# Key decay terms of an attention kernel: from tiles spread over the partitions to one more matmul per score tile

## The chip, the cores and the metric

The kernel runs on one core of a Trainium2 chip. The metric is the device time of one execution in microseconds; the times given are medians of several runs, and the profile is of one further execution.

## What is computed

Three layers follow each other: causal attention with a decay (4 batches, 8 heads, 576 positions, head width 64), a mixture of 8 experts with one expert per token (2304 tokens), and a feed-forward layer. Only the attention is touched by the change:

```python
scores = scale * np.matmul(q, k.transpose(0, 1, 3, 2))
log_f = np.log(np.clip(f, 0.0001, 1.0))
cum = np.cumsum(log_f, axis=-1)
decay = cum[:, :, :, None] - cum[:, :, None, :]
scores = np.where(causal, -1000000000.0, scores + decay)
scores = scores - np.max(scores, axis=-1, keepdims=True)
attn = np.exp(scores)
attn = attn / (np.sum(attn, axis=-1, keepdims=True) + 1e-09)
return np.matmul(attn, v).astype(np.float32)
```

The query's own term, `cum[:, :, :, None]`, is the same for a whole row and falls out of the softmax. What remains is a row over the keys, `-cum`, that is added to every row of a head's scores.

## The kernel before

**Units.** The heads are taken in 16 pairs (`gp`, four per batch), and each pair in six units (`SUB`, line 541): units 0 and 1 are the fourth row block of each head (128 queries by 512 keys), units 2 and 3 the third and the first block of one head (384 and 128 keys), unit 4 the second blocks of both heads (256 each), unit 5 the last 64 queries of both heads, stacked on the partitions, by 512 and 64 keys. 96 units run through a software pipeline (line 1322). Its step n issues `scores(n+2)`, `parts_hi` and `parts_lo` of n-1, `maxima(n+2)`, `values(n-3)`, `exps(n+1)` and `turn(n)`, and after them what the table `side` holds for the step: loads, splits, transposes and stores at steps that the numbers of `PRM` set by hand. Every engine's order, that of the DMA queue of SP too, is the order of these calls, and each engine works in order.

**Scores.** `scores` (line 552, TensorE) puts a unit's tile into one PSUM buffer `s`: for every piece of keys one matmul with the high half (`wcc`, line 566) and one with halves swapped (`yw`, line 567), then `identb` times `maskb` for the causal mask on the diagonal block (line 568). Queries and keys come in half a batch at a time (`hb`, eight of them, four heads each): `prep_load`, `prep` (split into two float16 parts), `prep_turn` (DMA transposes, line 313, into `wcc`) and `prep_swap` (line 353: two DMAs that write `yw`, the keys with the 64-row halves exchanged).

**Decay.** At the start `cum_log` and `cum_sums` (lines 424 to 440) compute -8 times the running sum for the 32 heads as a 32x576 float32 tile, and `cum_store` writes it to `cumd` in HBM. `cb_spread(gp)` (line 388) then reads it back for each pair, spread over partitions: `cb` holds both heads' first 512 values on all 128 partitions, `c4` one head's 576 on the lower and the other's on the upper 64. It is issued eight steps before the pair begins (line 921), 48 DMAs in all.

**Reductions.** `maxima` (line 599, VectorE) adds the spread tile to the scores, scales by -1/8, writes the float32 tile `e` and takes the row minimum into `nm` (line 608; lines 614 and 618 for unit 5). `exps` (ScalarE, line 631) makes `t`, `turn` transposes it on TensorE into `pt` (line 643), `parts_hi` (ScalarE) and `parts_lo` (VectorE, line 659) split that into `p`, and `values` (lines 694 and 708) multiplies with V. `normal` and `rows` (lines 720 and 736) make the finished rows `nat`, which `rows_store` writes to `xs` (line 769); there are two buffers of `nat`.

**Others in the same steps.** The routing of a batch (line 783 on, with scatters of 4-byte indices into `ids`), loads and splits of one expert's weights, and three early slots of 128 tokens of that expert (`xgt`, `hs`, `ht`) run between the units. Behind step 98 come the other expert slots and the feed-forward layer, which need the transfers of weights and are not touched.

Of the kernel before, what the change touches and what calls it, by code (L numbers as in the profile page):

```python
# [92 lines left out]
def kernel(  # L93
# [22 lines left out]
    P = 128  # L116
# [26 lines left out]
    cumd = dram.tile([B * H, S], F32, name="cumd")  # L143
# [5 lines left out]
    mask4 = const.tile([P, 64], BF16, name="mask4")  # L149
    ones16 = const.tile([P, P], F16, name="ones16")  # L150
# [237 lines left out]
    def cb_spread(gp):  # L388

        cb = cbp.tile([P, 2, 512], F32, tag="cb", name="cb")  # L390
        nc.sync.dma_start(out=cb, in_=cumd[2 * gp:2 * gp + 2, 0:512].partition_broadcast(P))

        c4 = cbp.tile([P, S], F32, tag="cb4", name="cb4")
        for a in range(2):
            nc.sync.dma_start(out=c4[64 * a:64 * a + 64, :], in_=cumd[2 * gp + a, :].partition_broadcast(64))
        cbs[gp] = (cb, c4)

    def identities():
        make_identity(nc, identf)
        nc.gpsimd.memset(maskb, 0.0)  # L400
        mh = maskb.rearrange("p (a c) -> p a c", a=2)
        nc.gpsimd.affine_select(
            out=mh, in_=mh, pattern=[[-1, 2], [-2, 64]], base=0, channel_multiplier=1,
            compare_op=ALU.is_ge, fill=-8.0e9,
        )
        nc.gpsimd.memset(mask4, 0.0)
        nc.gpsimd.affine_select(
            out=mask4, in_=mask4, pattern=[[-1, 64]], base=0, channel_multiplier=1,
            compare_op=ALU.is_ge, fill=-8.0e9,
        )  # L410
# [20 lines left out]
    def cum_sums():  # L431
# [8 lines left out]
        cum["cs"] = cs  # L440

    def cum_store():
        nc.sync.dma_start(out=cumd, in_=cum["cs"])
# [108 lines left out]
    def scores(u):  # L552
# [3 lines left out]
        h0 = 2 * (pr % 2)  # L556
        if SUB[x] is not None:
            ps = ps_s.tile([P, 512], F32, tag="s", name="s")
            for a, i, c0 in SUB[x]:
                w = i * P + P  # L560
                h = h0 + a
                lhs = t[:, i, 0, h, :]
                for (k0, kw, r0), (_, _, r1) in zip(keys(t[:, :, 1, h], i), keys(yt[:, :, h], i)):
                    last = k0 + kw == w
                    o = ps[:, c0 + k0:c0 + k0 + kw]
                    nc.tensor.matmul(o, lhsT=lhs, rhs=r0, start=True, stop=False)  # L566
                    nc.tensor.matmul(o, lhsT=lhs, rhs=r1, start=False, stop=not last)  # L567
                nc.tensor.matmul(ps[:, c0 + w - P:c0 + w], lhsT=identb, rhs=maskb, start=False, stop=True)  # L568
            U[u] = [ps]
        else:  # L570
            pb = ps_s.tile([P, 64], F32, tag="s", name="sb")
            pa = ps_s.tile([P, 512], F32, tag="s", name="sa")
            lhs = [t[:, 4, 0, h0 + a, 0:64] for a in range(2)]
            for r in range(2):
                for a in range(2):
                    h = h0 + a
                    rhs = t[:, 4, 1, h, 0:64] if r == 0 else yt[:, 4, h, 0:64]
                    nc.tensor.matmul(pb[64 * a:64 * a + 64, :], lhsT=lhs[a], rhs=rhs, start=(r == 0), stop=False)
# [4 lines left out]
            for z in range(2):  # L583
                for r in range(2):
                    for a in range(2):
                        k0, kw, rhs = keys(t[:, :, 1, h0 + a] if r == 0 else yt[:, :, h0 + a], 3)[z]
                        nc.tensor.matmul(
                            pa[64 * a:64 * a + 64, k0:k0 + kw], lhsT=lhs[a], rhs=rhs, start=(r == 0), stop=(r == 1)
# [10 lines left out]
    def maxima(u):  # L599
        gp, x = divmod(u, NU)  # L600
        cb, c4 = cbs[gp]
        e = ep.tile([P, S], F32, tag="e", name="e")
        nm = nmp.tile([P, 2], F32, tag="nm", name="nm")
        if SUB[x] is not None:
            ps, = U[u]
            for y, (a, i, c0) in enumerate(SUB[x]):
                w = i * P + P
                nc.vector.tensor_tensor_reduce(  # L608
                    out=e[:, c0:c0 + w], in0=ps[:, c0:c0 + w], in1=cb[:, a, 0:w], scale=-1.0 / 8.0, scalar=3.0e38,
                    op0=ALU.add, op1=ALU.min, accum_out=nm[:, y:y + 1],  # L610
                )
        else:
            pa, pb = U[u]
            nc.vector.tensor_tensor_reduce(  # L614
                out=e[:, 512:S], in0=pb, in1=c4[:, 512:S], scale=-1.0 / 8.0, scalar=3.0e38,
                op0=ALU.add, op1=ALU.min, accum_out=nm[:, 1:2],
            )
            nc.vector.tensor_tensor_reduce(
                out=e[:, 0:512], in0=pa, in1=c4[:, 0:512], scale=-1.0 / 8.0, scalar=nm[:, 1:2],
                op0=ALU.add, op1=ALU.min, accum_out=nm[:, 0:1],  # L620
# [297 lines left out]
    for gp in range(B * NPAIR):  # L918
        o = PRM["gp" + str(gp)]
        if gp > 0:  # L920
            at(6 * gp - 8, cb_spread, gp)
# [379 lines left out]
    cb_spread(0)  # L1301
# [443 lines left out]
```

## Time and profile before

| what | value |
|---|---|
| median of 3 runs | 973.28 us (970.16 to 973.96) |
| profiled execution | 972.13 us, its span 970.4 us |
| TensorE busy | 799.5 us (82%), 5373 matmuls |
| VectorE busy | 513.6 us (53%) |
| ScalarE busy | 346.9 us (36%) |
| GpSimd busy | 339.4 us (35%) |
| mean granted TensorE clock | 0.92 |
| DMA traffic | 116.12 MB in 233,424 packets |

The busy times are sums over the whole span; a matmul's time runs from its start to its modelled end, so matmuls that follow closely overlap. A DMA share is the mean busy share of the 16 DMA engines; it exceeds 1 where an engine has several packets in flight. A wait is the idle time of an engine just before an instruction, put down to what ended it. In the views TensorE is PE (its weight loads PEld), VectorE DVE, ScalarE ACT, GpSimd POOL, and SPq the sequencer of SyncE, which issues most DMAs.

### The profile page before, as it was taken

Reading aid. Unit: us, or ns where it says so; the run is one execution under the profiler, and the core shown is the slowest. Engines: PE = TensorE matmul, PEld = TensorE weight load, DVE = VectorE, ACT = ScalarE, POOL = GpSimd, SP = SyncE. Lnnn points to the kernel's source line nnn. Section 1 sums busy time; section 2 is a strip of 40 time slices with the busy share of each in tenths; the row PEclk is TensorE's granted clock in tenths of the full one; section 3 lists DMA queues with packets and bytes.
Section 4 is the critical chain, followed back from the end, with each engine's and each line's share of the span. In section 5 each row is a group of like instructions: output and inputs, shape, how many; then the busy total and the mean of one; then the engine's idle time right before and its main releaser. Section 6 shows DMA issues by size and latency. Waiting matters only on the chain. (4 is left out here: it accounts for less than half of the span.)

```text
span 970.4 us, 15407 instructions
## 1 busy us (share of the span) xinstructions
PE 799.5 (82%) x5373; PEld 445.4 (46%) x5373; DVE 513.6 (53%) x1231; ACT 346.9 (36%) x670; POOL 339.4 (35%) x383
## 2 busy tenths in 40 slices
PE   4676663665788878497998889999999999999995
PEld 3565552553556543143443337444444444444442
DVE  5776573764765644558899578935005304501500
ACT  4676453643655442344545333312102101201200
POOL 3333252234232442454555434534114303411410
PEclk9887796779879989799999899999999999999998
DMA  9999999999999279799998936202000200000000
GB/s 186 194 179 195 186 149 161 211 195 162 170 179 142 39 134 163 150 267 204 238 242 217 228 84 163 60 22 44 12 33 1 43 33 12 1 23 22 1 22 22
DMA packets 233424, 116.12 MB, mean 120 GB/s; under 512 B 193587, under 2 KB 214592, under 8 KB 233346
## 3 DMA queue, kind: packets, MB, share of 16 engines
q1 hardware_dynamic: 227810, 100.25, 58.2%
q0 software_dynamic: 5536, 14.86, 5.0%
q8 instruction: 45, 0.74, 0.3%
q14 instruction: 33, 0.27, 0.1%
HBM read 62.05 MB, written 15.56 MB: 80 GB/s over the span
## 5 line engine op out<-in xcount | busy, mean ns | idle before, releaser
L1647 PE MATMUL a<-x,wi 128*128 128x512 f16 x768 | 167.4, 380 | 0.0
L1652 DVE TENSOR_SCALAR t<-a,al 128x512 f32<-128x512 f32 (+1 forms) x80 | 55.7, 696 | 205.2 <-PE a L1647 204.4
L1647 PEld LDWEIGHTS <-wi 128*128 128x128 f16 x960 | 94.5, 99 | 98.6 <-issue 6.0
L1669 PEld LDWEIGHTS <-g 128*128 128x128 f16 x864 | 84.5, 98 | 104.1 <-issue 2.4
L1210 PE MATMUL y<-wcc,ht 128*128 (+1 forms) x456 | 110.3, 398 | 20.0 <-DMA ht<-hs 19.1
L1175 PE MATMUL h<-wcc,xgt 128*128 (+1 forms) x456 | 109.4, 396 | 20.2 <-POOL wcc L1377 14.5
L1660 POOL TENSOR_TENSOR g<-t,g 128x512 f16<-128x512 f32 (+1 forms) x80 | 85.6, 1072 | 113.8 <-ACT g L1659 110.9
L643 PE MATMUL pt<-identf,t 128*128 128x128 f32 x384 | 72.2, 318 | 61.3 <-ACT t L631 37.5
L1669 PE MATMUL o<-wo,g 128*128 128x512 f16 x540 | 119.5, 379 | 0.0
L1659 ACT ACTIVATE g<-t 128x512 f16<-128x512 f32 (+1 forms) x80 | 46.8, 586 | 154.7 <-DVE t L1655 150.0
L659 DVE SCALAR_TENSOR_TENSOR p<-pt,p 128x512 f16<-128x512 f32 x96 | 65.5, 683 | 43.9 <-ACT p L652 42.7
L631 ACT ACTIVATE t<-e,nm 128x512 f32<-128x512 f32 (+2 forms) x144 | 81.2, 601 | 15.7 <-DVE nm L608 8.9
L1210 PEld LDWEIGHTS <-ht 128*128 128x128 f16 x480 | 48.2, 101 | 83.4 <-DMA ht<-hs 26.1
L1175 PEld LDWEIGHTS <-xgt 128*128 128x128 f16 x480 | 47.9, 101 | 79.2 <-issue 22.0
L643 PEld LDWEIGHTS pt<-identf,t 128*128 128x128 f32 x384 | 47.4, 160 | 66.8 <-ACT t L631 55.1
L1669 PE MATMUL o<-wob,g 128*128 128x512 f16 x324 | 73.2, 379 | 1.8 <-POOL wob L1455 1.6
L1676 POOL DMA_INDIRECT out_dram<-ob,tka x18 | 17.6, 977 | 153.5 <-ACT ob L1674 153.5
L608 DVE CUSTOM_DVE_ANT_0 e<-s,cb 128x512 f32<-128x512 f32 (+3 forms) x128 | 58.2, 481 | 22.0 <-PE s L568 18.6
L567 PE MATMUL s<-yw,wcc 128*128 128x256 f16 (+1 forms) x192 | 50.7, 293 | 22.5 <-DMA yw<-wcc 22.5
L1674 ACT ACTIVATE ob<-o 128x512 f32<-128x512 f32 x18 | 10.8, 598 | 160.9 <-PE o L1669 160.9
L652 ACT ACTIVATE p<-pt 128x512 f16<-128x512 f32 x96 | 56.3, 587 | 7.3 <-PE pt L643 3.1
L566 PE MATMUL s<-wcc 128*128 128x256 f16 (+1 forms) x192 | 52.4, 292 | 6.1 <-DVE nm L614 2.5
(305 smaller groups left out, 1136.6 us busy)
## 6 DMA issues: line engine op xcount, KB each, us to landing
cb<-cumd SPq DMA_DIRECT2D x16, 512.0 KB
raw<-in_moe_w_in_dram SPq DMA_DIRECT2D x16, 512.0 KB
raw<-in_moe_w_out_dram SPq DMA_DIRECT2D x16, 512.0 KB
cb<-cumd SPq DMA_DIRECT2D x32, 144.0 KB
yw<-wcc SPq DMA_DIRECT2D x14, 320.0 KB
kn<-in_k_dram SPq DMA_DIRECT2D x16, 256.0 KB
qn<-in_q_dram SPq DMA_DIRECT2D x32, 128.0 KB
vn<-in_v_dram SPq DMA_DIRECT2D x16, 256.0 KB
```

What stands on the lines that cost most here:

```text
L566: nc.tensor.matmul(o, lhsT=lhs, rhs=r0, start=True, stop=False)
L608: nc.vector.tensor_tensor_reduce(out=e[:, c0:c0 + w], in0=ps[:, c0:c0 + w], in1=cb[:, a, 0:w], scale=-1.0 / 8.0, scalar=3.0e38, op0=ALU.ad ...
L631: nc.scalar.activation(out=natural(t[:, c0:c0 + w]), in_=halves(e[:, c0:c0 + w]), func=AF.Exp, scale=-1.0, bias=nm[:, y:y + 1])
L643: nc.tensor.transpose(pt[:, c * P:(c + 1) * P], e[:, c * P:(c + 1) * P], identf)
L652: nc.scalar.activation(out=p[:, 0, 0:512], in_=U[u][0], func=AF.Copy, scale=SP)
L659: nc.vector.scalar_tensor_tensor(out=p[:, 1, 0:512], in0=U[u][0], scalar=SP, in1=p[:, 0, 0:512], op0=ALU.mult, op1=ALU.subtract)
L1175: nc.tensor.matmul(hps, lhsT=xgt[:, kk, l, :], rhs=m1(m, kk, cs_), start=(kk == 0 and y == 0), stop=(kk == KD - 1 and y == 2),)
L1210: nc.tensor.matmul(yps, lhsT=ht[:, kk // (KF // 2), l, kk % (KF // 2), :], rhs=m2(m, kk), start=(kk == 0 and y == 0), stop=(kk == KF - 1 a ...
L1647: nc.tensor.matmul(hps[:, 0:n], lhsT=wi[:, mm, kk, m * P:(m + 1) * P], rhs=x2[:, l, kk, 0:n], start=(kk == 0 and y == 0), stop=(kk == KD - ...
L1652: nc.vector.tensor_scalar(out=t[:, 0:n], in0=hps[:, 0:n], scalar1=0.0, scalar2=al[:, m:m + 1], op0=ALU.min, op1=ALU.mult)
L1660: nc.gpsimd.tensor_tensor(out=g[:, 1, 0:n], in0=t[:, 0:n], in1=g[:, 0, 0:n], op=ALU.subtract)
L1669: nc.tensor.matmul(ops, lhsT=g[:, l, t * P:(t + 1) * P], rhs=wo[m // (KH - LATE)][:, mm, m % (KH - LATE), :], start=(m == 0 and y == 0), s ...
```

## The change

The decay row is no longer added by VectorE from a spread tile. `cum_sums` splits it into three bfloat16 parts (`c3`: cast, subtract, cast, subtract, cast), `cumd` holds these, and `cb_load(hb)` brings 3 rows of four heads (3x4x576 bfloat16) for half a batch at once, at step `6 * gp - 12` for even `gp`. In `scores` a matmul with `one3` (3x128 ones) as weights and the three parts as moving operand opens every tile's accumulation, over the whole width. The reductions become `tensor_scalar` instructions with the scores as their only tensor.

```diff
--- before.py
+++ after.py
@@ -140,13 +140,14 @@
     ys = dram.tile([N, YW], F16, name="ys")
     G0 = 256
     ids = dram.tile([(E * ROWS + 1) * P, 1], I32, name="ids")
-    cumd = dram.tile([B * H, S], F32, name="cumd")
+    cumd = dram.tile([B * H, 3, S], BF16, name="cumd")
 
     identf = const.tile([P, P], F32, name="identf")
     identb = const.tile([P, P], BF16, name="identb")
     identh = const.tile([P, P], F16, name="identh")
     maskb = const.tile([P, P], BF16, name="maskb")
     mask4 = const.tile([P, 64], BF16, name="mask4")
+    one3 = const.tile([3, P], BF16, name="one3")
     ones16 = const.tile([P, P], F16, name="ones16")
     before16 = const.tile([P, P], F16, name="before16")
     ef = const.tile([P, E], F32, name="ef")
@@ -385,15 +386,11 @@
 
     cbs = {}
 
-    def cb_spread(gp):
-
-        cb = cbp.tile([P, 2, 512], F32, tag="cb", name="cb")
-        nc.sync.dma_start(out=cb, in_=cumd[2 * gp:2 * gp + 2, 0:512].partition_broadcast(P))
-
-        c4 = cbp.tile([P, S], F32, tag="cb4", name="cb4")
-        for a in range(2):
-            nc.sync.dma_start(out=c4[64 * a:64 * a + 64, :], in_=cumd[2 * gp + a, :].partition_broadcast(64))
-        cbs[gp] = (cb, c4)
+    def cb_load(hb):
+
+        cb = cbp.tile([3, 4, S], BF16, tag="cb", name="cb")
+        nc.sync.dma_start(out=cb, in_=cumd[4 * hb:4 * hb + 4].rearrange("h r s -> r h s"))
+        cbs[hb] = cb
 
     def identities():
         make_identity(nc, identf)
@@ -403,6 +400,7 @@
             out=mh, in_=mh, pattern=[[-1, 2], [-2, 64]], base=0, channel_multiplier=1,
             compare_op=ALU.is_ge, fill=-8.0e9,
         )
+        nc.gpsimd.memset(one3, 1.0)
         nc.gpsimd.memset(mask4, 0.0)
         nc.gpsimd.affine_select(
             out=mask4, in_=mask4, pattern=[[-1, 64]], base=0, channel_multiplier=1,
@@ -437,10 +435,16 @@
             out=halves(cs[:, 0:512]), in0=natural(cu[:, 0:512]), scalar1=-8.0, scalar2=None, op0=ALU.mult
         )
         nc.vector.tensor_scalar(out=cs[:, 512:S], in0=cu[:, 512:S], scalar1=-8.0, scalar2=None, op0=ALU.mult)
-        cum["cs"] = cs
+
+        c3 = ep.tile([BH, 3, S], BF16, tag="c3", name="c3", bufs=1)
+        for r in range(3):
+            nc.vector.tensor_copy(c3[:, r], cs)
+            if r < 2:
+                nc.vector.tensor_tensor(out=cs, in0=cs, in1=c3[:, r], op=ALU.subtract)
+        cum["c3"] = c3
 
     def cum_store():
-        nc.sync.dma_start(out=cumd, in_=cum["cs"])
+        nc.sync.dma_start(out=cumd, in_=cum["c3"])
 
     sets = {}
 
@@ -554,28 +558,37 @@
         b, pr = divmod(gp, NPAIR)
         t, yt = xy[2 * b + pr // 2], yw[2 * b + pr // 2]
         h0 = 2 * (pr % 2)
+        cb = cbs[2 * b + pr // 2]
         if SUB[x] is not None:
             ps = ps_s.tile([P, 512], F32, tag="s", name="s")
             for a, i, c0 in SUB[x]:
                 w = i * P + P
                 h = h0 + a
                 lhs = t[:, i, 0, h, :]
+                nc.tensor.matmul(ps[:, c0:c0 + w], lhsT=one3, rhs=cb[:, h, 0:w], start=True, stop=False)
                 for (k0, kw, r0), (_, _, r1) in zip(keys(t[:, :, 1, h], i), keys(yt[:, :, h], i)):
-                    last = k0 + kw == w
                     o = ps[:, c0 + k0:c0 + k0 + kw]
-                    nc.tensor.matmul(o, lhsT=lhs, rhs=r0, start=True, stop=False)
-                    nc.tensor.matmul(o, lhsT=lhs, rhs=r1, start=False, stop=not last)
+                    nc.tensor.matmul(o, lhsT=lhs, rhs=r0, start=False, stop=False)
+                    nc.tensor.matmul(o, lhsT=lhs, rhs=r1, start=False, stop=False)
                 nc.tensor.matmul(ps[:, c0 + w - P:c0 + w], lhsT=identb, rhs=maskb, start=False, stop=True)
             U[u] = [ps]
         else:
             pb = ps_s.tile([P, 64], F32, tag="s", name="sb")
             pa = ps_s.tile([P, 512], F32, tag="s", name="sa")
             lhs = [t[:, 4, 0, h0 + a, 0:64] for a in range(2)]
+            for a in range(2):
+                c = cb[:, h0 + a]
+                nc.tensor.matmul(
+                    pb[64 * a:64 * a + 64, :], lhsT=one3[:, 0:64], rhs=c[:, 512:S], start=True, stop=False
+                )
+                nc.tensor.matmul(
+                    pa[64 * a:64 * a + 64, :], lhsT=one3[:, 0:64], rhs=c[:, 0:512], start=True, stop=False
+                )
             for r in range(2):
                 for a in range(2):
                     h = h0 + a
                     rhs = t[:, 4, 1, h, 0:64] if r == 0 else yt[:, 4, h, 0:64]
-                    nc.tensor.matmul(pb[64 * a:64 * a + 64, :], lhsT=lhs[a], rhs=rhs, start=(r == 0), stop=False)
+                    nc.tensor.matmul(pb[64 * a:64 * a + 64, :], lhsT=lhs[a], rhs=rhs, start=False, stop=False)
             for a in range(2):
                 nc.tensor.matmul(
                     pb[64 * a:64 * a + 64, :], lhsT=identb[:, 0:64], rhs=mask4, start=False, stop=True
@@ -585,7 +598,7 @@
                     for a in range(2):
                         k0, kw, rhs = keys(t[:, :, 1, h0 + a] if r == 0 else yt[:, :, h0 + a], 3)[z]
                         nc.tensor.matmul(
-                            pa[64 * a:64 * a + 64, k0:k0 + kw], lhsT=lhs[a], rhs=rhs, start=(r == 0), stop=(r == 1)
+                            pa[64 * a:64 * a + 64, k0:k0 + kw], lhsT=lhs[a], rhs=rhs, start=False, stop=(z == 1 and r == 1)
                         )
             U[u] = [pa, pb]
 
@@ -598,26 +611,25 @@
 
     def maxima(u):
         gp, x = divmod(u, NU)
-        cb, c4 = cbs[gp]
         e = ep.tile([P, S], F32, tag="e", name="e")
         nm = nmp.tile([P, 2], F32, tag="nm", name="nm")
         if SUB[x] is not None:
             ps, = U[u]
             for y, (a, i, c0) in enumerate(SUB[x]):
                 w = i * P + P
-                nc.vector.tensor_tensor_reduce(
-                    out=e[:, c0:c0 + w], in0=ps[:, c0:c0 + w], in1=cb[:, a, 0:w], scale=-1.0 / 8.0, scalar=3.0e38,
-                    op0=ALU.add, op1=ALU.min, accum_out=nm[:, y:y + 1],
+                nc.vector.tensor_scalar(
+                    out=e[:, c0:c0 + w], in0=ps[:, c0:c0 + w], scalar1=-1.0 / 8.0, scalar2=3.0e38,
+                    op0=ALU.mult, op1=ALU.min, accum_out=nm[:, y:y + 1],
                 )
         else:
             pa, pb = U[u]
-            nc.vector.tensor_tensor_reduce(
-                out=e[:, 512:S], in0=pb, in1=c4[:, 512:S], scale=-1.0 / 8.0, scalar=3.0e38,
-                op0=ALU.add, op1=ALU.min, accum_out=nm[:, 1:2],
+            nc.vector.tensor_scalar(
+                out=e[:, 512:S], in0=pb, scalar1=-1.0 / 8.0, scalar2=3.0e38,
+                op0=ALU.mult, op1=ALU.min, accum_out=nm[:, 1:2],
             )
-            nc.vector.tensor_tensor_reduce(
-                out=e[:, 0:512], in0=pa, in1=c4[:, 0:512], scale=-1.0 / 8.0, scalar=nm[:, 1:2],
-                op0=ALU.add, op1=ALU.min, accum_out=nm[:, 0:1],
+            nc.vector.tensor_scalar(
+                out=e[:, 0:512], in0=pa, scalar1=-1.0 / 8.0, scalar2=nm[:, 1:2],
+                op0=ALU.mult, op1=ALU.min, accum_out=nm[:, 0:1],
             )
         U[u] = [e, nm]
 
@@ -918,7 +930,8 @@
     for gp in range(B * NPAIR):
         o = PRM["gp" + str(gp)]
         if gp > 0:
-            at(6 * gp - 8, cb_spread, gp)
+            if gp % 2 == 0:
+                at(6 * gp - 12, cb_load, gp // 2)
         if gp < B * NPAIR - 1:
             at(min(6 * gp + o[2], 24 * B + 2), normal, gp)
             at(min(6 * gp + o[3], 24 * B + 2), rows, gp)
@@ -1298,7 +1311,7 @@
     prep_lo(0, 0)
     vload(0, 0)
     cum_store()
-    cb_spread(0)
+    cb_load(0)
     prep_first(0, 1)
     prep_hi(0, 1)
     prep_first(0, 0)
```

The order of the engines' instructions is otherwise that of before. On SP's queue, ahead of the first swap of keys (line 353, `yw`), the loads and transposes of half batch 1 stand with the spread of pair 2 among them. Before:

```order
L277 DMA kn<-in_k_dram 64x4x64
L279 DMA qn<-in_q_dram 64x4x64
L391 DMA cb<-cumd 128x2x512
L395 DMA cb_601<-cumd 64x576 x2
L313 DMA_TRANSPOSE wcc<-st 128x8x64
L272 DMA kn<-in_k_dram 128x4x128
L279 DMA qn<-in_q_dram 128x4x64 x2
L353 DMA yw<-wcc 64x5x512 x2
```

After:

```order
L278 DMA kn<-in_k_dram 64x4x64
L280 DMA qn<-in_q_dram 64x4x64
L314 DMA_TRANSPOSE wcc<-st 128x8x64
L273 DMA kn<-in_k_dram 128x4x128
L280 DMA qn<-in_q_dram 128x4x64 x2
L354 DMA yw<-wcc 64x5x512 x2
```

The three DMAs of the spread are gone from between the loads and the transpose; the small load of this half batch stands further ahead in the queue.

On TensorE, the first unit's tile `s` (`wcc` are the queries and keys, `one_69` is `one3`). Before:

```order
L566 LDWEIGHTS wcc
L566 MATMUL s<-wcc 128x256
L567 LDWEIGHTS wcc
L567 MATMUL s<-yw,wcc 128x256
L566 LDWEIGHTS wcc
L566 MATMUL s<-wcc 128x256
```

After:

```order
L568 LDWEIGHTS one_69
L568 MATMUL s<-cb,one_69 128x512
L571 LDWEIGHTS wcc
L571 MATMUL s<-wcc 128x256
L572 LDWEIGHTS wcc
L572 MATMUL s<-yw,wcc 128x256
```

A weight load and a matmul over the tile's whole width stand first, so the first instruction of a tile now reads `cb`.

On VectorE, at the start of the program, after the running sum `cu`. Before:

```order
L436 TENSOR_SCALAR cs<-cu 32x512
L439 TENSOR_SCALAR cs<-cu 32x64
L301 TENSOR_TENSOR st<-qn,st 128x2x4x64
L338 COPY wcc<-tp 128x512 x2
L255 CAST st<-kn 128x2x4x64
```

After:

```order
L437 TENSOR_SCALAR cs<-cu 32x64
L441 CAST c_226<-cs 32x576
L443 TENSOR_TENSOR cs<-cs,c_226 32x576
L441 CAST c_226<-cs 32x576
L443 TENSOR_TENSOR cs<-cs,c_226 32x576
L441 CAST c_226<-cs 32x576
L302 TENSOR_TENSOR st<-qn,st 128x2x4x64
L339 COPY wcc<-tp 128x512 x2
```

Five instructions stand ahead of the subtraction `st` of the first queries, whose transposes TensorE does next.

## Rows read from the trace of the kernel before

**Rows 1.** Busy time by stretch; clock, DMA share and GB/s stand last.

```profile
14.00:346.00 332.00, 226.35 (x2583) 176.49 (x2581) 210.35 (x698) 181.63 (x406) 117.72 (x146) 0.83 1.06 167
```

**Rows 2.** The page: 40 slices of the span, then the line of SP's queue.

```profile
DMA  9999999999999279799998936202000200000000
GB/s 186 194 179 195 186 149 161 211 195 162 170 179 142 39 134 163 150 267 204 238 242 217 228 84 163 60 22 44 12 33 1 43 33 12 1 23 22 1 22 22
...
q1 hardware_dynamic: 227810, 100.25, 58.2%
```

**Rows 3.** The page's DMA issues: the spread of the decay.

```profile
cb<-cumd SPq DMA_DIRECT2D x16, 512.0 KB
...
cb<-cumd SPq DMA_DIRECT2D x32, 144.0 KB
```

**Rows 4.** Waits in 14 to 346 us: total, times, longest.

```profile
PE s L567 <- DMA yw<-wcc: 22.5, 4, 6.6
ACT nat L253 <- DMA xs<-nat: 20.5, 3, 14.9
...
ACT hs L1182 <- DMA ht<-hs: 18.7, 2, 13.2
...
PE pt L643 <- DVE p L659: 16.2, 10, 4.4
...
ACT x L253 <- DMA xs<-x: 8.0, 2, 5.0
...
DVE e L608 <- DMA cb<-cumd: 2.6, 1, 2.6
```

**Rows 5.** Timeline of SP, 68 to 83 us: start, duration, instruction.

```profile
71.51 0.55 SPq L391 DMA_DIRECT2D cb<-cumd  x1
...
75.44 2.62 SPq L353 DMA_DIRECT2D yw<-wcc  x2
```

**Rows 6.** Timeline of PE, 71 to 84 us.

```profile
75.47 0.27 PE L566 MATMUL s<-wcc 128*128 128x256 f16 x1
82.34 0.39 PE L567 MATMUL s<-yw,wcc 128*128 128x256 f16 x1 [6.60 <-DMA yw<-wcc]
```

**Rows 7.** Matmul prices: chain of waits; groups in 14:346; timeline of PE, 257 to 268.

```profile
649.74 31.08 PE a L1647 x144
...
L708 PE MATMUL xp<-v,p 128*128 128x130 f16 x120 | 14.8, 238 | 0.0
...
L708 PE MATMUL xp<-v,p 64*128 64x130 f16 x30 | 5.6, 237 | 0.0
...
259.70 0.28 PE L587 MATMUL sa<-yw,wcc 128*64 128x256 f16 x2
259.81 0.28 PE L587 MATMUL sa<-wcc 128*64 128x256 f16 x2
```

**Rows 8.** Groups of VectorE by form: busy, mean ns, idle before.

```profile
L1652 DVE TENSOR_SCALAR t<-a,al 128x512 f32<-128x512 f32 x64 | 48.0, 750 | 201.0 <-PE a L1647 201.0
...
L608 DVE CUSTOM_DVE_ANT_0 e<-s,cb 128x512 f32<-128x512 f32 x32 | 21.9, 684 | 19.6 <-PE s L568 16.9 <-DMA cb<-cumd 2.6
...
L618 DVE CUSTOM_DVE_ANT_0 e<-sa,cb,nm 128x512 f32<-128x512 f32 x16 | 12.0, 751 | 2.4 <-PE sa L587 0.2
...
L608 DVE DVE_READ_ACCUMULATOR2_ANT nm<- 128x1 f32 x128 | 10.3, 80 | 0.0
```

**Rows 9.** Timeline of the start, 0 to 24 us.

```profile
7.82 0.67 DVE L301 TENSOR_TENSOR st<-qn,st 128x512 f16<-128x512 f32 x1
7.92 0.33 SPq L443 DMA_DIRECT2D cumd<-cs  x1
...
9.09 0.40 DVE L255 CAST st<-kn 128x512 f16<-128x512 f32 x1
...
10.31 0.36 SPq L391 DMA_DIRECT2D cb<-cumd  x1
...
15.16 0.69 DVE L608 CUSTOM_DVE_ANT_0 e<-s,cb 128x512 f32<-128x512 f32 x1 [0.64 <-PE s L568]
```

## The prediction

> **What bounds the kernel now.** I began with the busy table by stretch. From 14 to 346 us the program runs attention; in this stage [rows 1] no engine is full: TensorE has a matmul in flight for 226 of 332 us, VectorE is busy 210, ScalarE 182. The granted TensorE clock is 0.83 on average, a mix of its two levels, 2.4 and 1.2 GHz. What is full is the transfer side: the DMA share is 1.06, and the line of slices on the page [rows 2] shows a 9 in each of the first 13 slices of 24 us. So I looked at what the idle time ends on. Waits for transfers [rows 4]: 22.5 us for the swapped keys (yw), 20.5 for the store of the attention rows (ScalarE may not overwrite nat before it has landed), 18.7 for ht, 8.0 for xs<-x, 2.6 for the spread tiles themselves: 72 us in 12 waits. The engines stand one behind the other in such a hole, so this is close to stage time. In these waits the queue matters more than the operand. At 71.5 us SP begins to issue the three DMAs of a spread, then come other transfers, then at 75.4 the swap [rows 5]; TensorE begins the score tile at 75.47 and sits idle 6.60 us until 82.34 [rows 6]. The spread stands in front of the late transfer. Behind 346 us nothing is touched; I let that part move with the end of attention.
>
> **The terms.** I work on the profiled execution: 972.13 us, 1.2 under the median of the runs (973.28).
>
> *Transfers.* Removed: 16 spreads, each of one 512 KB and two 144 KB DMAs [rows 3], 819,200 bytes, 13.1 MB in all; that is 24% of what the stage moves (332 us at 167 GB/s is 55 MB, rows 1). Eight small loads of 12 rows of 1152 bytes take their place; 14 KB each, twelve steps ahead of need, I cost at nothing: if one came late, TensorE's score tile would wait for it, in order, with everything behind. SP also issues 40 DMAs less. What does a spread cost those behind it? The queue's own line [rows 2] gives two ends: 227,810 packets and 100.25 MB took 58.2% of 970 us, 565 us. By packets (a spread is 256 + 128 of them) that is 0.95 us, by bytes (177 GB/s) 4.6 us. I take 3.1 us, 819,200 bytes at the 267 GB/s of the best slice [rows 2], since long pieces should move better than the mean. Twelve waits, each shorter by 3.1: **-37 us**; ends -11 and -55.
>
> By the Trainium skill (DMA: Bandwidth & Descriptors, Specifications) transfers of 512 bytes and more run at line rate, up to 435 GB/s, so these pieces of 2 KB would cost least of all here: an estimate of 1.9 us a spread, 23 us in all, and the sum below would be 967 instead of 953. No slice of this trace goes above 267 GB/s.
>
> *TensorE.* Added per pair of heads: a matmul over the whole width of every score tile. Units 0 and 1 have 512 columns each, units 2 and 3 384 + 128, unit 4 twice 256, unit 5 two of 64 and two of 512: 3,712 columns, 59,392 over 16 pairs, in 192 matmuls. That the weights have three rows saves nothing: 64 rows took 237 ns where 128 took 238 [rows 7]. The price of 512 columns comes from the chain, 144 matmuls in 31.08 us, 0.216 us each, at full clock: 25.0 us. At the stage's mean clock of 0.83 it is 30. Unit 5's four may cost less: the two heads write different halves of the partitions, and such pairs of 256 columns started every 0.11 us [rows 7], the time of one. The 192 weight loads run ahead beside matmuls, as those of the other score matmuls do. How much of the 30 is path? TensorE is in order, and it waits 107 us of 332 now, of which DVE's p alone ends 16.2 [rows 4]; what lies in such waits is absorbed, and a decay matmul that stands ahead of a late swap costs nothing. I take two thirds, **+20 us**; ends +8 and +30.
>
> *VectorE.* The 160 reductions lose their second operand, and one instruction takes the place of two. The separate read-out of the accumulator was 80 ns [rows 8]: 160 x 80 = 12.8 us less. The main instruction: 684 ns for 512 columns before; the nearest TENSOR_SCALAR out of PSUM took 750 (L1652), but with a pointer operand, and the old form with a pointer (L618) also took 751. Without one I take 684 again; the other end is 66 ns more, 160 times, +10.6. VectorE ends a minor part of the waits, so I count 40% of 12.8: **-5 us**; ends -13 and +11.
>
> By the Trainium skill (VectorE: DVE Perf Modes, Two Vector instructions with no wait between them) an op that also writes out its accumulator is two instructions, the main one and an accumulator read. By that rule the read-outs stay, the term is nothing and the sum 958. The order of the changed program lists one row per reduction; no row of the trace before has this form.
>
> *Start.* VectorE gets three casts and two subtractions of 32x576 ahead of prep_lo: with 0.40 us for a cast and 0.67 for a subtraction of 512 columns [rows 9], longer by 576/512, 2.8 us. Behind them stand the subtraction that the first transposes wait for, and the store of cumd, which today goes out at 7.92 and lets the spread start at 10.31 [rows 9]. The load now gates TensorE's first score rather than VectorE's first reduction, but it is small, and the V and K loads behind it are relieved of 819 KB. **+2.5 us**; ends 0 and +5.
>
> *Nothing:* the memset of one3 (GpSimd, idle in the first microseconds), the buffer of 3x4x576 (the old tiles were larger).
>
> Sum: -37 + 20 - 5 + 2.5 = -19.5; 972.1 - 19.5 = **953 us**. Late next: TensorE itself, and transposes behind the stores.
>
> **Rivals.**
>
> *The queue is paid by the packet.* The trace's packets are mostly short, and 384 long ones are little among 227,810. Then each wait shrinks by 0.95 us, 11 us in all: 972 - 11 + 20 - 5 + 2.5 = 979. For it: the chains of transpose, swap and score stay, and each link has its own delay. Against it: the spread directly ahead of the swap in rows 5.
>
> *TensorE becomes the bound: slower.* Of TensorE's 107 idle microseconds the waits for transfers make up to 72, so outside them it has little room, and it leaves a hole at the low clock (the matmul at 82.34 in rows 6 takes 0.39 us, the one before the hole 0.27). If the holes stay, so does the low clock, and the 30 us all land on the path: 972 + 30 + 2.5 - 11 = 994. VectorE's gain is then worth nothing. With the whole 30 the kernel is slower wherever the transfer term is under 32 us. Against it: a hole that stays is also a place where added matmuls cost nothing.
>
> *The queue paces the whole stage.* Its share is above 1 nearly throughout, so every byte removed is time: -55, the matmuls fall into waits (+8), VectorE -5, start +2.5: 972 - 50 = 923. Against it: several waits of rows 4 (x, ht) come where stores and scatters of a few bytes stand in the queue, which stay.
>
> *The change may not do what it says* at one place, the read-out; it is the end of a term above, not a case of its own.
>
> **How the numbers follow.** My forecast has 0.58, its own range 938 to 968 (the transfer term from -50 to -24). Paid by the packet 0.14, TensorE bound 0.10, queue as pace 0.18. A measurement of this kernel tells about 0.5% from no change, here 968 to 978. Faster: 0.18, and 0.55 of my case: 0.73. Same: 0.03 of mine, 0.09 of the packet case, 0.01: 0.13. Slower: 0.14. The range for 8 in 10 takes my case, half of the pace case and most of the packet case: 920 to 980.
>
> **What would show it.** In the changed profile: yw waits of TensorE at about 10 us instead of 22.5, the store's wait shorter by as much as a spread; the DMA share of the stage still near 1, its bytes down to about 42 MB; the end of attention near 326 us instead of 346; a granted clock above 0.83; 192 matmuls with one3 spaced 0.21 us at full clock; VectorE's busy time down by about 13 us, or not, if read-outs still stand behind the reductions; the first reduction near 17 to 18 us instead of 15.2. I am wrong if the waits for transfers stay above 55 us in all, or if TensorE's idle time in the stage doesn't fall below 80 us.

## The result and the profile after

The changed kernel takes 941.36 us, the median of 4 runs (940.68 to 942.79); the kernel before, run beside it, 971.92 us. The ratio is 0.9687, 95% interval 0.9661 to 0.9713: 30.6 us faster. I had forecast 19.5.

Where the time went is shown by the last score tiles. The transposes of the exponentials, 384 in each kernel, are the last work of every unit; the view of their line gives the first and last start, ahead in the kernel before, then in the changed one.

```profile
L643 PE MATMUL pt<-identf,t x384: 272/273/477, 22.5 to 346.9; 128*128 128x128 f32 x192
```

```profile
L655 PE MATMUL pt<-identf,t x384: 272/273/474, 23.8 to 317.3; 128*128 128x128 f32 x192
```

Attention ends 29.6 us sooner, though its first unit starts 1.3 us later. Behind it lie 623.5 us before (span 970.4) and 622.1 after (span 939.4): that part moved along, as assumed. The busy times of the stretch to that end answer to [rows 1]:

```profile
14.00:317.00 303.00, 265.83 (x2806) 177.89 (x2806) 215.17 (x701) 185.00 (x409) 118.96 (x153) 0.89 0.87 145
```

TensorE has work in flight for 266 of 303 us, where it had 226 of 332; the granted clock rose from 0.83 to 0.89; the DMA share fell from 1.06 to 0.87, and the bytes from 55 to 44 MB (303 us at 145 GB/s). The page's queue line, against [rows 2]:

```profile
q1 hardware_dynamic: 221018, 87.29, 49.6%
```

The waits of the same stretch answer to [rows 4] (total us, times, longest):

```profile
PEld L568 <- issue: 21.3, 87, 0.8
...
PEld L571 <- issue: 15.8, 70, 0.4
...
PE y L1223 <- DMA ht<-hs: 11.1, 2, 7.1
ACT nat L254 <- DMA xs<-nat: 8.9, 2, 7.7
...
PE s L572 <- DMA yw<-wcc: 3.2, 1, 3.2
```

The swapped keys are waited for 3.2 us in place of 22.5, the row store 8.9 in place of 20.5; the waits for xs<-x, for the spread and ScalarE's for hs (18.7) are gone. TensorE's for ht grew from 1.9 to 11.1. New are the two lines on top: the weight loads (PEld) of the decay matmul (L568) and of the matmul behind it (L571) stand idle 37 us in 157 short pieces that end on no other engine. "Issue" means that nothing the profile shows was waited for. The timeline of TensorE in an undisturbed unit shows one such piece on either side of the decay matmul (start, duration):

```profile
57.91 0.63 PE L655 MATMUL pt<-identf,t 128*128 128x128 f32 x4
58.47 0.09 PEld L568 LDWEIGHTS <-one 3*128 3x128 bf16 x1 [0.17 <-issue]
58.47 0.38 PE L568 MATMUL s<-cb,one 3*128 3x512 bf16 x1
...
58.78 0.10 PEld L571 LDWEIGHTS <-wcc 128*128 128x128 f16 x1 [0.23 <-issue]
58.79 0.28 PE L571 MATMUL s<-wcc 128*128 128x256 f16 x1
58.80 0.10 PEld L572 LDWEIGHTS <-wcc 128*128 128x128 f16 x1
58.91 0.27 PE L572 MATMUL s<-yw,wcc 128*128 128x256 f16 x1
```

The weights of L572 load while L571's matmul streams, 0.01 us behind its start. The weights of L571 load only when the 512 columns of the decay have run, and the decay's own only when the transposes have. So the next matmul starts 0.32 us behind the decay matmul, where its columns take 0.216 [rows 7], and the decay matmul itself starts late.

The kernel before already had such a place. In `values` (L708) three loads of 64-row weights follow twelve of 128 rows, 15 times in 14 to 346 us (busy us, mean ns, idle before):

```profile
L708 PEld LDWEIGHTS <-p 128*128 128x128 f16 x180 | 12.8, 107 | 0.3
...
L708 PEld LDWEIGHTS <-p 64*128 64x128 f16 x45 | 2.7, 98 | 1.9 <-issue 0.6
```

The weight loads stand idle 0.3 us in all before the 180 loads of 128 rows and 1.9 us before the 45 of 64 rows, some 0.13 us for each change to 64 rows.

VectorE's groups by form (busy us, mean ns) answer to [rows 8]:

```profile
L620 DVE TENSOR_SCALAR_CACHE_REDUCE e<-s 128x512 f32<-128x512 f32 x32 | 21.8, 681 | 4.4 <-PE s L573 4.4
...
L630 DVE TENSOR_SCALAR_CACHE_REDUCE e<-sa,nm 128x512 f32<-128x512 f32 x16 | 12.0, 750 | 2.4 <-PE sa L600 0.6
...
L620 DVE DVE_READ_ACCUMULATOR e<-s 128x1 f32 x128 | 10.2, 80 | 0.0
```

681 ns against 684, 750 against 751, and the read-out of 80 ns is still there. At the start, VectorE's rows against [rows 9]:

```profile
10.68 0.67 DVE L302 TENSOR_TENSOR st<-qn,st 128x512 f16<-128x512 f32 x1
...
18.55 0.69 DVE L620 TENSOR_SCALAR_CACHE_REDUCE e<-s 128x512 f32<-128x512 f32 x1 [1.18 <-PE s L573]
```

The subtraction of prep_lo starts 2.9 us later than before (7.82), the first reduction 3.4 us later (15.16).

### The profile page after: what moved, and what is told of

Read it like the earlier page. It is cut to its first block, busy times and chain, and to the rows that moved or that the text cites. A ratio compares the mean times of both kernels' runs of the same rounds, so it can differ in the third digit from the quotient of the medians.

```text
span 939.4 us, 15722 instructions
## 1 busy us (share of the span) xinstructions
PE 837.1 (89%) x5565; PEld 444.4 (47%) x5565; DVE 525.8 (56%) x1236; ACT 348.6 (37%) x670; POOL 340.7 (36%) x384
## 5 line engine op out<-in xcount | busy, mean ns | idle before, releaser
L655 PE MATMUL pt<-identf,t 128*128 128x128 f32 x384 | 68.1, 305 | 11.8 <-ACT t L643 8.2
L620 DVE TENSOR_SCALAR_CACHE_REDUCE e<-s 128x512 f32<-128x512 f32 (+3 forms) x128 | 58.1, 480 | 8.1 <-PE s L573 8.1
L1668 DVE SCALAR_TENSOR_TENSOR t<-a,t 128x512 f32<-128x512 f32 (+1 forms) x80 | 51.0, 638 | 2.7
L655 PEld LDWEIGHTS pt<-identf,t 128*128 128x128 f32 x384 | 45.2, 154 | 14.6 <-ACT t L643 9.1
L572 PE MATMUL s<-yw,wcc 128*128 128x256 f16 (+1 forms) x192 | 48.2, 277 | 3.2 <-DMA yw<-wcc 3.2
```

The costliest lines, as they stand in the source:

```text
L620: nc.vector.tensor_scalar(out=e[:, c0:c0 + w], in0=ps[:, c0:c0 + w], scalar1=-1.0 / 8.0, scalar2=3.0e38, op0=ALU.mult, op1=ALU.min, accum_ ...
L655: nc.tensor.transpose(pt[:, c * P:(c + 1) * P], e[:, c * P:(c + 1) * P], identf)
L1668: nc.vector.scalar_tensor_tensor(out=t[:, 0:n], in0=hps[:, 0:n], scalar=0.0, in1=t[:, 0:n], op0=ALU.max, op1=ALU.add)
```

## The experiments

Twelve runs of eleven kernels were made in three groups, each group on one chip beside the kernel before. The chips differ by over a per cent (before: 983.65, 971.84 and 983.67 us), so times of different groups are compared by their ratios to before. Two kernels leave decay terms out or wrong, and their tokens may go to other experts; there the end of attention is looked at beside the time. An end of attention comes from one trace, and two traces of one kernel on two of the chips ended 13 us apart (311.4 and 298.3, full rows).

**Theories.** Mine: the spreads' bytes were what others waited for, and the decay matmuls cost more than their columns, because weights of 3 rows aren't loaded beside a neighbour of 128. Rivals: the price of the columns; the number of transfers, or of their pieces; VectorE.

### 1. Weights of 128 rows

```diff
-    one3 = const.tile([3, P], BF16, name="one3")
+    one3 = const.tile([P, P], BF16, name="one3")
...
+    cbz = [cbp.tile([P, 4, S], BF16, tag="cb" + str(j), name="cb" + str(j), bufs=1) for j in range(2)]
...
+        nc.gpsimd.memset(cbz[0].bitcast(F32), 0.0)
...
-        cb = cbp.tile([3, 4, S], BF16, tag="cb", name="cb")
-        nc.sync.dma_start(out=cb, in_=cumd[4 * hb:4 * hb + 4].rearrange("h r s -> r h s"))
+        cb = cbz[hb % 2]
+        nc.sync.dma_start(out=cb[0:3], in_=cumd[4 * hb:4 * hb + 4].rearrange("h r s -> r h s"))
```

> The kernel after the change, with decay weights of 128 rows in place of 3: one3 is 128 x 128 ones and the tile that it meets has rows 3 to 127 at zero (two standing tiles, zeroed once; the transfers still bring 3 rows). The same columns, the same sums. Theory (weight loads uncovered): in the kernel after, the weights of 3 rows are not loaded beside the matmul ahead of them, nor the 128-row weights behind them; the idle time of the weight loads at the decay line (21.3 us of issue) and at the line behind it (15.8 us) goes, TensorE is busy about 30 us less before 316 us, and with two thirds of that on the path the attention ends some 20 us sooner: 941 - 20 = 921 us, 912 to 930. Rival 1 (columns): the price is that of the streamed columns, so it stays: 939 to 944. Rival 2 (not TensorE): the gaps go, but transfers or VectorE end the stage: 933 to 940, with TensorE's busy time down by 25 us or more all the same.

Measured: 940.49 us, ratio 0.956 (0.9515 to 0.9604). Attention ended at 311.4 us, 6 sooner than in the changed kernel, with TensorE busy 233 us instead of 266. That could be rival 2, or the chip, so it ran again beside the changed kernel itself:

> The kernel after the change once more, unaltered, so that it, the full-row weights and the versions below stand against each other on one chip. Every theory expects its ratio to the kernel before as it was, 0.966 to 0.971.

> The full-row weights once more, beside the kernel after on one chip. The first run's trace showed TensorE busy 33 us less before the end of attention and the attention ending 6 us sooner. Theory (the uncovered weight loads cost the path 6 us, the rest of the 33 lay beside waits for transfers): 4 to 8 us under the kernel after on this chip. Rival (they cost nothing, the first run's 6 us were another chip's): within 2 us of it.

Measured on one chip: the changed kernel 941.38 us, ratio 0.9656 (0.9601 to 0.9711); full rows 930.65 us, 0.9598 (0.9556 to 0.9639). The medians are 10.7 us apart, the ratios 5.6 us of 972; the two intervals just overlap. Over both groups full rows stand at 0.956 and 0.960, three rows at 0.966 and 0.969. The full-row kernel's weight loads to the end of attention (the second trace), then its busy times and timeline:

```profile
L573 PEld LDWEIGHTS <-wcc 128*128 128x128 f16 x192 | 20.2, 105 | 7.4 <-issue 3.4
...
L570 PEld LDWEIGHTS <-one 128*128 128x128 bf16 x128 | 13.3, 104 | 5.7 <-DVE e L622 2.1 <-issue 1.2
```

```profile
14.00:298.00 284.00, 231.01 (x2806) 181.20 (x2806) 217.12 (x701) 184.00 (x409) 119.58 (x155) 0.92 0.93 154
```

```profile
58.26 0.63 PE L657 MATMUL pt<-identf,t 128*128 128x128 f32 x4
58.73 0.38 PE L570 MATMUL s<-cb,one 128*128 128x512 bf16 x1
58.94 0.27 PE L573 MATMUL s<-wcc 128*128 128x256 f16 x1
```

The idle time of issue falls from 37.1 to 4.6 us, the matmul behind the decay starts 0.21 us after it (0.32 with 3 rows), the decay matmul 0.47 us after the transposes (0.56). Same columns, same sums: the gaps come from the row count. By the ratios they cost 6 to 12 us of time, by the medians on one chip 10.7; the rest of the 33 us of busy time did not show in the time. With full rows two waits for transfers are longer, 12.8 us for the row store (8.9) and 6.1 for the swapped keys (3.2); a third, TensorE's for ht, is 1.8 us (11.1).

### 2. Weights of 32 and of 64 rows

```diff
-    one3 = const.tile([P, P], BF16, name="one3")
+    one3 = const.tile([32, P], BF16, name="one3")
```

The standing tiles get 32 rows as well, or 64.

> As the full-row weights, with 32 rows (three of terms, 29 of zeros). One look at TensorE: idle time of the weight loads at the decay line and at the line behind it, 37 us of issue with 3 rows and some 4 with 128, and TensorE's busy time to the end of attention, 266 us with 3 rows and 233 with 128. Theory (a switch to weights of another row count is what isn't covered): idle time over 30 us, busy 255 or more. Rival (only an odd count that leaves a part of TensorE's rows in use together with others is at fault): under 10 us of idle time, busy 230 to 240.

> The same with 64 rows. Theory (any other row count than its neighbours' 128): as with 3 rows, over 30 us of idle time, busy 255 or more. Rival (a matter of how few the rows are): idle time between that of 3 and of 128 rows, busy 238 to 252.

Measured in one execution each: 948.46 and 942.77 us (before: 983.67). The weight loads to the end of attention, of 32 rows and of 64:

```profile
L573 PEld LDWEIGHTS <-wcc 128*128 128x128 f16 x192 | 19.1, 100 | 24.4 <-issue 17.5 <-ACT yw L342 0.2
...
L570 PEld LDWEIGHTS <-one 32*128 32x128 bf16 x128 | 11.8, 92 | 25.0 <-issue 20.6 <-DVE e L628 0.5 <-DVE e L622 0.3
```

```profile
L573 PEld LDWEIGHTS <-wcc 128*128 128x128 f16 x192 | 18.9, 99 | 22.4 <-issue 15.3 <-ACT yw L342 0.4 <-DMA yw<-wcc 0.2
...
L570 PEld LDWEIGHTS <-one 64*128 64x128 bf16 x128 | 12.0, 94 | 24.5 <-issue 19.6 <-DVE e L622 0.5 <-DVE e L628 0.5
```

Idle for issue: 37.1 us with 3 rows, 38.1 with 32, 34.9 with 64, 4.6 with 128. TensorE busy: 266, 261, 259, 231. With 32 and with 64 rows the matmul behind the decay starts 0.31 and 0.32 us after it. Each count below the neighbours' 128 leaves the gap; both rivals fall. These kernels have the standing tiles as well, so it isn't the tiles that close it.

### 3. Old spreads beside the new decay

```diff
+    d2 = cbp.tile([P, 1024], F32, tag="d2", name="d2", bufs=1)
+    d4 = cbp.tile([P, 512], F32, tag="d4", name="d4", bufs=1)
...
+        nc.sync.dma_start(
+            out=d2.rearrange("p (a c) -> p a c", a=2), in_=fv[2 * gp:2 * gp + 2, 0:512].partition_broadcast(P)
+        )
+        for a in range(2):
+            nc.sync.dma_start(out=d4[64 * a:64 * a + 64, :], in_=fv[2 * gp + a, 0:512].partition_broadcast(64))
...
+            at(6 * gp - 8, dummy, gp)
```

fv is the input f with its batches and heads on the rows; c3 shares d2's memory.

> The kernel after the change, and at the steps of the old spreads three transfers that nothing reads, of the old form: two rows of 512 float32 to all 128 partitions, and one row to 64 partitions twice (512 columns here, 576 then). Shows what the absence of the spreads is worth with everything else as changed. My forecast's term was 37 us (11 if paid by the packet at 0.95 us a spread, 55 if by bytes at 4.6 us). Theory (transfers in the queue's way): the wait for yw, 3.2 us in the kernel after, comes back to 15 or more, and the time rises by 35 to 60: 976 to 1001 us. Rival (TensorE has become the bound behind them): the transfers now hide beside TensorE's longer work, and only 5 to 20 come back: 946 to 961. Rival 2 (the gain came from VectorE or the order): under 5: 941 to 946.

Measured: 972.77 us, ratio 0.9899 (0.9832 to 0.9966), 2.1 to 2.4% above the changed kernel's ratios, 21 to 24 us. Between theory and first rival, nearer the rival. The wait for the swapped keys came back to 10.1 us, where the theory wanted 15. That wait, the busy times, and the transposes' first and last start:

```profile
PE s L583 <- DMA yw<-wcc: 10.1, 3, 5.3
```

```profile
14.00:347.00 333.00, 270.38 (x2805) 180.51 (x2805) 218.17 (x700) 185.00 (x409) 119.17 (x152) 0.85 1.01 167
```

```profile
L666 PE MATMUL pt<-identf,t x384: 272/273/476, 23.3 to 347.5; 128*128 128x128 f32 x192
```

Attention ends where it did before the change (346.9, on another chip), at the same 167 GB/s, with TensorE busy 44 us longer, and by the ratio this kernel is not slower than the one before. It has 15 spreads in place of 16, each 4% smaller. While the transfers set the pace, the decay matmuls, gaps and all, cost the stage nothing that shows.

### 4. Half the bytes, and hardly any

```diff
-            nc.sync.dma_start(out=d4[64 * a:64 * a + 64, :], in_=fv[2 * gp + a, 0:512].partition_broadcast(64))
+            nc.sync.dma_start(out=d4[64 * a:64 * a + 64, 0:256], in_=fv[2 * gp + a, 0:256].partition_broadcast(64))
```

So, and the transfer into d2 likewise, pieces of 1 KB in place of 2 KB. In the second kernel each of the three is `fv[..., 0:16].partition_broadcast(16)`, 16 pieces of 64 bytes.

> The same with as many pieces as the full-size spreads have (two rows to 128 partitions, and one to 64 partitions twice), each of 1 KB in place of 2 KB: half the bytes. Theory (bytes): about half of what the full size gave back, 0.975 to 0.981, the attention ends near 332 us. Rival 1 (paid by the piece, whatever its length): as full size, 0.986 to 0.994, the end near 345. Rival 2 (issues alone): as the tiny transfers'.

> The kernel after the change and, at the old steps, three transfers a pair that nothing reads, each of 16 pieces of 64 bytes: the old spreads' number of issues and places in SP's queue with nearly none of their bytes. With full-size spreads the ratio to before was 0.990, without them 0.966 to 0.969. Theory (the bytes of the spreads are what the others waited for): 0.964 to 0.973, the attention ends near 318 us. Rival (issues and the few transfers that SP's queue has under way at once): most of the 22 us comes back, 0.980 or more, the end near 340.

Measured: 961.47 us, ratio 0.9798 (0.9747 to 0.9849), and 951.01 us, 0.9676 (0.9622 to 0.9729). The tiny transfers cost nothing that shows against the changed kernel's 0.966 to 0.969, half the bytes about 12 us, all of them about 22: in step with the bytes. Half and full size have the same number of issues and of pieces, and their intervals overlap by a hair, on two chips; the tiny ones have the same issues but far fewer pieces, so they rule out the issues and not the pieces. The single traces end attention at 331 us (half) and 328 (tiny, where 318 was expected), which tells the two apart less well than the medians do.

### 5. The old kernel without its spreads

```diff
-            at(6 * gp - 8, cb_spread, gp)
+            cbs[gp] = None
...
-        cb, c4 = cbs[gp]
+        cb, c4 = cbs[0]
```

> The kernel before the change with the first spread alone: every pair of heads reads the decay terms of pair 0 (so the decay of the others is left wrong, and the token's experts may come out otherwise). VectorE's reductions with the tile from memory stay, TensorE has no decay matmul, 15 of 16 spreads are gone. Theory (my forecast's terms by themselves: transfers 37, ends 11 and 55): 972 - 37 = 935, 917 to 961. Theory now (the transfers were worth 50 or more, the decay matmuls took back 20 to 30): 905 to 922, with the wait for yw at most 5 us in place of 22.5. Rival (VectorE's other operation, not the transfers): 960 to 972. Against the run without decay matmuls: the same within 5 us if the two kinds of reduction cost VectorE the same; 8 to 13 slower if the read-outs or the second operand counted.

Measured: 937.04 us, ratio 0.9527 (0.9477 to 0.9576): of 972 us that is 46, 41 to 51, for 15 spreads, without any decay matmul. Attention ended at 312.1 us; its busy times and the wait for the swapped keys:

```profile
14.00:312.00 298.00, 225.83 (x2583) 175.77 (x2582) 214.02 (x700) 181.38 (x408) 118.54 (x147) 0.85 1.01 147
```

```profile
PE s L567 <- DMA yw<-wcc: 5.9, 2, 4.4
```

46 lies between the 37 of my forecast and the 50 or more that I supposed by then; the wait for the swapped keys is just above the 5 us expected. What follows attention took 626.7 us here and 627.5 and 630.9 in experiments 3 and 1 on the same chip, so the total can be used although the decay terms are wrong. The kernel with full-row decay matmuls (0.956 and 0.960) is 3 to 7 us above it, its later start included; the intervals overlap, so this is not clear of noise.

### 6. The changed kernel without decay matmuls

```diff
-                nc.tensor.matmul(ps[:, c0:c0 + w], lhsT=one3, rhs=cb[:, h, 0:w], start=True, stop=False)
...
-                    nc.tensor.matmul(o, lhsT=lhs, rhs=r0, start=False, stop=False)
+                    nc.tensor.matmul(o, lhsT=lhs, rhs=r0, start=True, stop=False)
```

Unit 5 likewise, as before the change.

> The kernel after the change without its decay matmuls: the decay terms are left out of the scores altogether (the mask stays), the three-row tile is still loaded and nobody reads it. The token's experts may so come out otherwise, so that the attention stage before 316 us counts, not the total alone. Theory (decay matmuls cost the path some 30 us, through 52 us of busy TensorE): the stage ends 25 to 35 us sooner, and the time is 905 to 918. Rival 1 (my forecast's +20 on the path): 918 to 925. Rival 2 (TensorE covers nothing, transfers end the stage): 932 to 941.

Measured: 976.43 us, ratio 0.9929 (0.9896 to 0.9962); attention ended at 305.0 us. What follows it was 51 us longer than in the changed kernel, so the total tells nothing here. The busy times of the stage:

```profile
14.00:305.00 291.00, 220.86 (x2617) 173.77 (x2618) 217.54 (x702) 183.49 (x410) 120.81 (x154) 0.88 0.93 150
```

The stage ended 12 us sooner than with three-row decay matmuls (317.3, another chip): between rival 2 (0 to 9) and rival 1 (16 to 23), and not the 25 to 35 of the theory. Two traces of one kernel lie as far apart, so this doesn't choose between the rivals. It speaks against the theory: TensorE is busy 45 us less than in the changed kernel (265.83), and most of that does not show in the stage's end. Against the old reductions without spreads (312.1) and the full rows (311.4), both on its own chip, it ended 6 to 7 us sooner, too little for single traces to tell anything.

### 7. Towards a faster version

Full rows and a third buffer for nat, then also the first heads' terms sent directly:

```diff
-        nat = xnp.tile([P, 4, 2, 2, D], F16, tag="nat", name="nat")
+        nat = xnp.tile([P, 4, 2, 2, D], F16, tag="nat", name="nat", bufs=3)
```

```diff
+        if hb == 0:
+            for h in range(4):
+                nc.sync.dma_start(out=cb[0:3, h], in_=cum["c3"][h:h + 1])
+            return cbs.setdefault(hb, cb)
...
-    cum_store()
     cb_load(0)
+    cum_store()
```

> Full-row weights, and a third buffer for nat, whose cast waits 10.6 us once for a store of the rows two pairs back. Theory (each such wait stands by itself on the path): the attention ends 7 to 10 us sooner than with the full-row weights alone, near 303 us, and the time falls as much. Rival (transfers end the stage, whose share is 0.93 of the DMA engines' time): the wait turns up at another reader of transfers (yw, ht, qn) and the time stays within 3 us of the full-row weights'.

> As the run with the third nat buffer, and at the start the first four heads' decay terms go straight from their tile to the tile of three rows in four transfers; the store for the later heads comes behind them. Theory (the store's landing ahead of the load is on the start's path): the first reduction starts 1.5 to 2.5 us sooner than 18.5 us, and the time falls by 1 to 2.5 us. Rival (what is gained ahead of the first units is lost at their first wait for a transfer): the first reduction moves, the attention's end and the time do not, within 1 us.

Measured: 927.27 us, ratio 0.955 (0.9505 to 0.9595), and 928.05 us, 0.9574 (0.9532 to 0.9616). Both have a lower median than the changed kernel on their chip (941.38 us); neither can be told from the full rows alone (930.65). With the third buffer the wait for the row store is gone, and the wait for the swapped keys, 6.1 us with full rows, is

```profile
PE s L574 <- DMA yw<-wcc: 11.2, 3, 6.7
```

which is what the rival says: the hole moves to the next late transfer. More than that it doesn't show: the time is 3.4 us under the full rows' by the medians, between the theory's 7 to 10 and the rival's 3, and TensorE's wait for ht, 11.0 us here, was 10.0 and 1.8 in the two traces of the full-row kernel. With the direct transfers the first reduction starts at 18.45 us, no sooner. TensorE's timeline there shows why:

```profile
11.59 1.04 PE L331 MATMUL tp<-identh,st 128*128 128x128 f16 x8 [4.33 <-DVE st L303]
...
16.03 1.06 PE L334 MATMUL tp<-identh,st 128*64 128x128 f16 x16
17.02 0.61 PE L574 MATMUL s<-cb,one 128*128 128x512 bf16 x1
```

The first decay matmul follows straight on the transposes; these waited for prep_lo's subtraction on VectorE, which stands behind the five new operations. So the load was not the gate. The third-buffer version has the lowest median of its group; it can't be told from the other two with full rows.

## Why the prediction was right

The direction and the range (920 to 980) held, and so did the main step, that the spreads' bytes in the queue's way are what the stage gets back. The sum was 11 us short, and two of its steps did not hold: the size of the transfer term, and the weight loads that run ahead. By terms, with ratios turned into us of 972:

- **Transfers, -37 forecast.** Measured -46 (experiment 5) where TensorE has no added work. There the waits of [rows 4] that I had added up fell from 72 us to 28 (row store 12.6, xs<-x 6.4, swapped keys 5.9, hs 2.7), by 45 us, about as much as the time: that such waits are close to stage time held. What failed is one spread for each of twelve waits. Over the 15 spreads 46 us is 3.07 us each, against the 3.1 that I took, but that agreement may be luck: no run shows 267 GB/s as the reason (the stage without spreads moves 147 GB/s), and beside the long decay matmuls the spreads cost only 22 us, 1.5 each. In that every spread counts, the rival "The queue paces the whole stage" was nearer, with too high a price. That bytes and not issues or packets are paid for was assumed; experiments 3 and 4 now show it, the part on packets by a narrow margin.
- **TensorE, +20 forecast.** About +15, from two errors of opposite sign. "The 192 weight loads run ahead beside matmuls, as those of the other score matmuls do" failed: 37 us of gaps, some 6 to 12 of them on the path. The trace before could have told: I compared the durations of 64 and 128 rows [rows 7], which are alike, and not the idle time of their loads (L708 above). The columns, of which I put two thirds of 30 us on the path, cost about 5 (3 to 7, the start included, not clear of noise): full rows keep TensorE busy 233 and 231 us where it is 226 with no decay matmul, at a granted clock of 0.90 and 0.92 against 0.85. A higher clock may have paid for part of the added work. How much is not shown, since the clock was 0.88 in experiment 6 with no decay matmul either.
- **VectorE, -5 forecast.** Nothing: the read-outs still stand at 80 ns, the main operations cost the same within 3 ns. The rule that I weighed and didn't follow, of the Trainium skill (VectorE: DVE Perf Modes, Two Vector instructions with no wait between them), that an operation which writes out its accumulator is two instructions, agrees with the trace.
- **Start, +2.5 forecast.** The first reduction came 3.4 us later, for the reason given (five operations on VectorE ahead of prep_lo, 2.9 us); the first transposes of a score tile only 1.3 us later. What that cost in time was not measured by itself.

Sum: -46 + 5 + 10 = -31, the start in the 5; measured -30.6. The three are successive differences between the same kernels, so that they add up is no evidence of its own. The slower rival, TensorE as the bound, came partly true: TensorE's 266 of 303 us are close to full, which is likely why taking the gaps out helped. It did not decide: it needed the whole 30 us of columns on the path, and about 15 came, gaps included.

Of the signs: the swapped keys' wait 3.2 us (near 10 forecast), the row store's 8.9 (20.5 before), bytes 44 MB (42), end of attention 317 (326), clock 0.89 (above 0.83), TensorE idle 37 us (106 before, under 80 forecast); of the waits for transfers that I had added up 12 us are left, 23 with TensorE's for ht (above 55 would have made me wrong). Wrong were the DMA share near 1 (0.87), the spacing of 0.21 us (0.32), and the first reduction at 17 to 18 us (18.55).

## What to carry to other kernels

Where the transfer engines are full for a whole stage, the waits that a profile shows are a poor count of what a removed transfer is worth: one spread for each of twelve waits gave 37 us, and taking out 15 spreads gave 46. An added small matmul is priced by what its weights do to the pipeline, as much as by its columns: give it the row count of its neighbours, by zeros if need be, and look at the weight loads' idle time, which may show the price before anything is changed. And what a change costs on one engine depends on whether the other bound is still there: the same decay matmuls left the stage's end where it was beside the spreads, and cost some 15 us without them.

## What the runs showed that I had not expected

A weight load of another row count than its neighbours' isn't covered, whether 3, 32 or 64 rows against 128: 0.1 us on either side, though the load itself takes 92 to 94 ns against 104. The Trainium skill (TensorE: Matmul & The Clock Gate, LDWEIGHTS (loading the stationary operand)) says that a load's time goes by the columns and not by the rows; the trace nearly agrees for the load, and shows that the spacing does not follow it. The Trainium skill (TensorE: Matmul & The Clock Gate, The mechanism) says that a load overlaps a matmul in flight only where their row groups differ, and names a background weight buffer as another way for a load to be pulled ahead. Of the row groups these runs show the opposite: 128 rows behind 128 overlap (L572 above), 32 behind 128 do not. The measurement decides. Which buffer a load went to no run shows, and why the hardware does so stays open.

The granted clock does not simply go up with TensorE's work. Without spreads it was 0.85 and 0.88 with no decay matmul (experiments 5 and 6), 0.89 with three rows, and 0.90 and 0.92 with full rows; beside the old spreads it was 0.85 with three rows, though TensorE was busy 270 us there.
